# A fused attention, routing and two-layer MoE kernel: early weight chunks, index columns by matmul, and MoE2 in groups of 512 tokens

## The chip, the cores and the metric

The kernel runs on one core of one Trainium2 chip. The metric is the time of one execution in microseconds (us) of device time; several executions are timed, and their median counts. A profile of one execution shows what each engine did: PE (TensorE, the matmuls) with PEld (its weight loads), DVE (VectorE), ACT (ScalarE), POOL (GpSimd), SP (SyncE, which here only issues DMAs) and the DMA engines.

## The reference

Three stages follow each other on 2304 tokens (4 sequences of 576) of 512 features. The first is a sliding-window attention with 8 heads of 64 and a linear bias, whose window is 128 positions. The second sends every token to one of 8 experts, with at most 288 tokens per expert, in the order of the gate's values; the expert is a two-layer network. The third is a dense two-layer network with x * sigmoid(x) between.

```python
def _moe_ref(x, w_gate, w1, w2):
    N, D = x.shape                      # 2304, 512
    cap = N // E                        # 288
    logits = x @ w_gate
    order = np.argsort(-logits.flatten())
    ...                                 # greedy: best (token, expert) pair first, an expert takes cap tokens
    for e in range(E):
        mask = assigned == e
        h = np.maximum(x[mask] @ w1[e], 0.0)
        out[mask] = h @ w2[e]

def _moe2_ref(x, w_in, w_out):          # 512 x 2048, 2048 x 512
    h = x @ w_in
    g = h * (1.0 / (1.0 + np.exp(-h)))
    return g @ w_out
```

All of it is float32. Where the matmuls need the precision, the kernel splits an operand in two (a rounded part, `hi`, and the remainder, `lo`) and adds three products: hi x hi, hi x lo and lo x hi. One such product is one matmul instruction in the type fp32r.

## The kernel before, in words

**Order.** The kernel is written as one stream of operations and a scheduler puts them in an order on each engine, by its own estimate of the times. An operation may move ahead of earlier ones when its data and buffers are ready. `keep_in_program_order` (the `keep` in the code) holds an instruction behind the one written before it on its engine. Each engine and SP's queue then work strictly in the order that the scheduler fixed, and an instruction that waits holds everything behind it.

**Attention** (L80 to L265) goes over 18 tiles `t` of 128 tokens, each in two halves `g` of four heads, 36 halves `2t + g`. For each half, PE makes the scores, DVE adds the bias and takes the maximum, ACT makes the exponentials, PE transposes them (L240), ACT copies them out (L242), POOL selects the two parts of the window (`pp` and `pc`, L246 and L248), and PE multiplies with the values (L255). DVE normalises (L258 to L261) and the tile goes to the DRAM table `xtab` (L263). At the end of each tile `first_choices` (L47) makes, on DVE, the columns `fb` and `gt` (L69, L71) that a matmul (L74) adds up for the routing.

**Routing** (L333) finds the thresholds by a chain of small operations, mostly on DVE with short matmuls between; L384 is one of the wider. Dummy matmuls (`k.busy`, L309) run beside. `slots` (L496) ends in `idx96`: 24 columns of 96 token numbers, in the order of the experts' slots. `pi` is the PSUM tile that holds them before the addition of a constant.

**Weights** (L541). MoE1 has 64 chunks of 128 x 1024 float32 (512 KB), one for each expert and each eighth of the hidden features; `fetch` loads a chunk into one of four `raw` buffers (L559, on SP), casts it on ACT (L561) and subtracts on POOL (chunks 0 to 6) or DVE (L562) into one of five `ring` buffers. The first four chunks are fetched between the attention and the routing, their cast and subtraction held in program order. MoE2 has 16 chunks that come as int64, 1 MB each; `fetch64` (L566) loads each in two halves and unpacks them with five DVE operations and two ACT operations a half (L577 to L584). Nine of these are unpacked during MoE1 into the pool `keep`, two near its end into the ring, five during the first block of MoE2.

**MoE1** (L625). For each expert, three indirect DMAs on POOL gather 96 tokens each from `xtab` (L639), PE transposes them and they are split. For each of 8 slices `f` of hidden features there are 12 matmuls into `p` (L659) and 12 into the four accumulators `y0` to `y3` (L589 to L591), each of 288 columns. When an expert is done its four accumulators are copied to `yT`, which keeps all of y^T in SBUF (L680, L682). At expert 2, `by128` (L821) writes `idx96` to the DRAM table `itab` and reads it back as `idx128`, the same numbers in 18 columns of 128, which the output's scatter needs.

**MoE2** (L711) goes over nine blocks of 256 tokens. `split_block` (L601) splits a block of `yT`. A step `f` (16 a block) has 12 matmuls of 256 columns (`part0`, L617), the sigmoid on ACT (L761), a multiplication on DVE (L762), the cast on ACT (L771), the subtraction on DVE (L772), and, one step later, six matmuls of 512 columns into two of the four accumulators (L721). A finished block is copied out (L729, L731) and scattered to the output by token number (L733). The accumulators of even and odd blocks take different PSUM banks.

## Time and profile before

| what | value |
|---|---|
| median of 3 runs | 839.61 us (838.45 to 839.8) |
| the profiled execution's own time | 844.54 us |
| its span, first to last instruction | 842.8 us |
| DMA traffic | 90.32 MB in 34795 packets, 9184 of them under 512 bytes |
| HBM read and written | 79.87 MB and 9.45 MB |
| mean granted clock of PE | 0.979 |

The span is roughly: attention to 156 us, routing to 192 us, the first gather to 200 us, MoE1 to about 430 us, MoE2 to 833 us, and the last scatter. Each row of the views below gives an engine, a line of the code, what is written and what is read (`out<-in`), and the shape. A row of the stretches has PE, PEld, DVE, ACT and POOL, each as busy time with its number of instructions. The clock is the share of full speed that PE was granted.

Two things help in reading. Matmuls are pipelined, so the distance between their starts is their cost and not the length of one; and a busy PE can still be slow, so the number of matmuls in a stretch of known pace says more than the busy time.

### The profile page before, as it was taken

The page shows a single profiled execution, that of the slowest core. Times are in us where ns is not written, and L with a number is a line of the kernel's source. Part 1 is how long each engine was busy: PE and PEld are TensorE (multiplying, and loading weights), DVE is VectorE, ACT ScalarE, POOL GpSimd, SP SyncE. Part 2 cuts the span into 40 slices and gives each one's busy share as a digit, 9 for nine tenths or more (in the row PEclk, how much of TensorE's full clock was granted, in tenths as well). Part 3 has the DMA queues.
Part 4 walks back from the last instruction along what each step waited for, and adds up shares of the span by engine and source line. Part 5 has one row for each costly group of instructions (what it writes and reads, how often), then busy time and mean ns, then how long its engine had stood idle before and what let it go on. Part 6 is the DMA issues. An engine that isn't in the chain of part 4 may idle for free.

```text
span 842.8 us, 14810 instructions
## 1 busy us (share of the span) xinstructions
PE 802.4 (95%) x5599; PEld 734.5 (87%) x5599; DVE 495.1 (59%) x1325; ACT 368.4 (44%) x773; POOL 191.0 (23%) x202
## 2 busy tenths in 40 slices
PE   7989999688999699999999999999999999999997
PEld 5889999447999699999997899999999999999996
DVE  7978898772786487888799733234333333333332
ACT  4857776302554365555554423223332323232222
POOL 3869797604202002000003300000000000000000
PEclk8999999997999799999999999999999999999999
DMA  9997782312678677766434100000000000000000
GB/s 228 278 254 213 203 230 80 117 35 80 213 241 122 182 245 226 226 209 228 140 118 127 57 18 5 21 1 26 1 26 1 26 1 26 2 26 1 23 4 25
DMA packets 34795, 90.32 MB, mean 107 GB/s; under 512 B 9184, under 2 KB 9824, under 8 KB 34720
## 3 DMA queue, kind: packets, MB, share of 16 engines
q1 hardware_dynamic: 31744, 79.89, 33.1%
q0 software_dynamic: 2976, 9.44, 3.7%
q8 instruction: 46, 0.75, 0.4%
q14 instruction: 29, 0.24, 0.1%
HBM read 79.87 MB, written 9.45 MB: 106 GB/s over the span
## 4 chain that ended last, share of the span: by engine, by line
PE 56%; DVE 9%; DMA 8%; issue 2%; ACT 2%; POOLq 0%; ACTq 0%; SPq 0%
PE y L721 21%; DMA raw<-w 8%; PE p L659 6%; PE p L589 4%; PE p L591 4%; PE p L590 4%; PE pt L589 4%; PE pt L590 4%; PE pt L591 4%; DVE w L562 2%; PE y L590 2%; PE y L591 2%; PE y L589 2%; DVE bits L579 2%; DVE bits L578 1%
## 5 line engine op out<-in xcount | busy, mean ns | idle before, releaser
L721 PE MATMUL y<-w,gh 128*128 128x512 f32 x548 | 192.4, 395 | 0.1
L772 DVE TENSOR_TENSOR gl<-s,gh 128x256 fp32r<-128x256 f32 x137 | 60.1, 439 | 90.1 <-ACT gh L771 89.3
L721 PE MATMUL y<-w,gl 128*128 128x512 f32 x274 | 108.4, 396 | 2.1 <-DVE gl L772 1.7
L721 PEld LDWEIGHTS y<-w,gh 128*128 128x128 f32 x548 | 94.8, 190 | 10.1 <-ACT gh L771 0.8
L771 ACT CAST gh<-s 128x256 fp32r<-128x256 f32 x137 | 55.5, 407 | 96.5 <-PE y L721 69.3
L733 POOL DMA_INDIRECT out<-raw,idx x18 | 17.4, 966 | 344.2 <-ACT raw L731 323.0
L561 ACT CAST w<-raw 128x1024 fp32r<-128x1024 f32 x64 | 66.9, 1049 | 64.8 <-DMA raw<-w 45.0
L562 DVE TENSOR_TENSOR w<-raw,w 128x1024 fp32r<-128x1024 f32 x57 | 69.6, 1222 | 36.7 <-ACT w L561 36.7
L659 PE MATMUL p<-xh,w 128*128 128x288 f32 x512 | 81.6, 300 | 8.1 <-DVE hl L663 7.8
L659 PEld LDWEIGHTS p<-xh,w 128*128 128x128 f32 x512 | 72.0, 190 | 9.9 <-DVE hl L663 9.7
L590 PE MATMUL y<-hl,w 128*128 128x288 f32 x256 | 75.2, 298 | 0.0
L591 PE MATMUL y<-hh,w 128*128 128x288 f32 x256 | 74.7, 297 | 0.0
L589 PE MATMUL y<-hh,w 128*128 128x288 f32 x256 | 70.6, 301 | 0.0
L762 DVE TENSOR_TENSOR s<-p,s 128x256 f32<-128x256 f32 x72 | 30.5, 423 | 66.2 <-ACT s L761 66.1
L762 DVE TENSOR_TENSOR s<-pt,s 128x256 f32<-128x256 f32 x72 | 30.4, 423 | 63.6 <-ACT s L761 61.4
L721 PEld LDWEIGHTS y<-w,gl 128*128 128x128 f32 x274 | 51.5, 188 | 12.7 <-DVE gl L772 3.8
L761 ACT ACTIVATE s<-p 128x256 f32<-128x256 f32 x72 | 27.6, 384 | 72.9 <-PE p L591 66.1
L761 ACT ACTIVATE s<-pt 128x256 f32<-128x256 f32 x72 | 27.6, 384 | 70.2 <-PE pt L591 66.4
L232 ACT ACTIVATE pe<-sc,mx 128x128 f32<-128x128 f32 x144 | 47.6, 394 | 18.8 <-DVE mx L230 18.5
L639 POOL DMA_INDIRECT xg<-xtab,idx x24 | 26.2, 1092 | 128.1 <-PE pt L643 122.7
L255 PE MATMUL po<-va,pp 128*128 128x73 f32 x256 | 49.1, 274 | 0.5 <-DVE m L51 0.4
L255 PE MATMUL po<-va,pc 128*128 128x73 f32 x256 | 49.4, 275 | 0.0
(205 smaller groups left out, 2148.2 us busy)
## 6 DMA issues: line engine op xcount, KB each, us to landing
raw<-w SPq DMA_DIRECT2D x96, 512.0 KB, 4.1
kr<-kT SPq DMA_DIRECT2D x35, 256.0 KB, 5.0
va<-vA SPq DMA_DIRECT2D x18, 292.0 KB, 5.2
qr<-qT SPq DMA_DIRECT2D x18, 256.0 KB, 5.8
vt<-vT SPq DMA_DIRECT2D x18, 256.0 KB, 5.2
xtab<-xt SPq DMA_DIRECT2D x18, 256.0 KB, 4.8
xg<-xtab,idx POOLq DMA_INDIRECT x24, 4.7
out<-raw,idx POOLq DMA_INDIRECT x18, 2.7
```

Of the source, the lines that this page charges most:

```text
L255: nc.tensor.matmul(po[:, j, :], w[:, j, :], va[:, s, 4 * g + j, :], start=(i == 0), stop=(i == nb - 1))
L561: keep(nc.scalar.copy(hi, r))
L562: keep((nc.vector if i > 6 else nc.gpsimd).tensor_tensor(lo, r, hi, ALU.subtract))
L589: nc.tensor.matmul(out, whi, xhi, start=start, stop=False)
L590: nc.tensor.matmul(out, whi, xlo, start=False, stop=False)
L591: nc.tensor.matmul(out, wlo, xhi, start=False, stop=stop)
L659: nc.tensor.matmul(p, w[:, dc * P:dc * P + P], x[:, dc, :], start=(i + dc == 0), stop=(i == 2 and dc == DC - 1))
L721: mm = nc.tensor.matmul(a, g[:, w], x[:, 512:], start=(f + i == 0), stop=(f == FC2 - 1 and i == 2))
L761: nc.scalar.activation(s, p, AF.Sigmoid)
L762: nc.vector.tensor_tensor(s, p, s, ALU.mult)
L771: nc.scalar.copy(gh, s)
L772: nc.vector.tensor_tensor(gl, s, gh, ALU.subtract)
```

## The change

Four things change.

The first four chunks of MoE1 are loaded by `load_early` (written into tiles 12 to 15 of the attention) and split by `split_early` (written behind the halves 31 to 34, cast on ACT and subtraction on POOL, in program order). All other chunks are subtracted on DVE. The fifth is fetched at the start of MoE1.

`by128` no longer goes through DRAM. `slots` copies `pi` to `cent` (float16) on ACT, a constant `shift` (96 x 288) is loaded and copied at the end of the attention, and six matmuls of 6 columns move the 96-row columns into 128-row columns; one DVE operation adds the constant.

y^T is no longer kept in SBUF. The copies of an expert's accumulators go to `yo`, and one DMA on SP writes it to the DRAM tensor `yd`. `load_group` reads a group of 512 tokens back, and `split_group` splits it in four parts. The group after the current one is read at the start of each group.

MoE2 runs over four groups of 512 tokens and one of 256. `part0` has 12 matmuls of 512 columns; for each step there are 12 matmuls of 512 columns into all four accumulators (6 in the last group). The accumulators have one set of banks. Nine int64 chunks are unpacked in MoE1, and seven (`LATE`) in the first group of MoE2, all subtractions on DVE.

```diff
+EARLY = (31, 32, 33, 34)
...
+        if NT - 6 <= t < NT - 2:
+            wts.load_early()
...
             next(later)
+            if 2 * t + g in EARLY:
+                wts.split_early()
...
+        nc.scalar.copy(k.cent, pi)
         nc.vector.tensor_scalar_add(idx96, pi, float(N // 2))
...
+    def load_early(self):
+        r = self.raw.tile([P, 1024], F32, name="raw")
+        self.tc.nc.sync.dma_start(r, self.w32[self.next + len(self.raws)])
+        self.raws.append(r)
+
+    def split_early(self):
+        nc, keep = self.tc.nc, self.tc.keep_in_program_order
+        r = self.raws.pop(0)
+        hi, lo = self.parts(self.ring)
+        keep(nc.scalar.copy(hi, r))
+        keep(nc.gpsimd.tensor_tensor(lo, r, hi, ALU.subtract))
+        self.ready[self.next] = hi, lo
+        self.next += 1
...
-            keep((nc.vector if i > 6 else nc.gpsimd).tensor_tensor(lo, r, hi, ALU.subtract))
+            nc.vector.tensor_tensor(lo, r, hi, ALU.subtract)
...
-            (nc.vector if i < 11 else nc.gpsimd).tensor_tensor(lo[:, s], f, hi[:, s], ALU.subtract)
+            nc.vector.tensor_tensor(lo[:, s], f, hi[:, s], ALU.subtract)
...
-BT = 256
-NB = N // BT
+BT = 512
+GROUPS = [(o, min(BT, N - o)) for o in range(0, N, BT)]
 LAG = 7
-LATE = (0, 2, 4, 6, 8)
+SOON = 9
+LATE = (0, 1, 3, 4, 6, 7, 9)
...
+def load_group(tc, pool, yd, g, width=BT):
+    o, n = GROUPS[g]
+    r = pool.tile([P, DC, width], F32, name="yr", bufs=1)
+    tc.nc.sync.dma_start(r[:, :, :n], yd.rearrange("c p n -> p c n")[:, :, o:o + n])
+    return r
+
+def split_group(tc, pool, r, g):
+    o, n = GROUPS[g]
+    yh, yl = (pool.tile([P, DC, BT], F32R, name=x, bufs=1)[:, :, :n] for x in ("yh", "yl"))
+    for c in range(DC):
+        tc.nc.scalar.copy(yh[:, c], r[:, c, :n])
+        tc.nc.vector.tensor_tensor(yl[:, c], r[:, c, :n], yh[:, c], ALU.subtract)
+    return yh, yl
...
             if f == FC1 - 1:
+                yo = m1.tile([P, DC, CAP], F32, name="yo", bufs=1)
                 for d in range(DC):
...
+                nc.sync.dma_start(yd.rearrange("c p n -> p c n")[:, :, e * CAP:(e + 1) * CAP], yo)
+        wts.fetch(5)
         gather(0)
...
-                if n + 3 >= E * FC1 and 9 + n + 3 - E * FC1 < FC2 - len(LATE):
-                    wts.fetch64(9 + n + 3 - E * FC1, wts.ring)
...
+                if e == E - 1 and f == 1:
+                    r0 = load_group(tc, yg, yd, 0)
                 if e == E - 1 and f == 3:
-                    y0 = split_block(tc, [...], yT, 0)
+                    y0 = split_group(tc, yg, r0, 0)
...
-                accs[b] = [py.tile([P, 512], F32, name=f"y{b % 2 * 2 + d}") for d in range(2)]
+                accs[g] = [py.tile([P, 512], F32, name=f"y{d}") for d in range(nd)]
...
+                yh, yl = split_group(tc, m2 if g % 2 else yg, r, g)
+            if g < last_g:
+                r = load_group(tc, yg, yd, g + 1)
...
-                s = m2.tile([P, BT], F32, name="s")
+                s = m2.tile([P, n], F32, name="s", bufs=1)
...
-    def by128():
-        tc.keep_in_program_order(nc.sync.dma_start(itab.rearrange("(j r) o -> r (j o)", r=JR), idx96))
-        nc.sync.dma_start(idx128, itab.rearrange("(c p) o -> p (c o)", p=P))
+    def by128(pi):
+        cent = k.cent.rearrange("r (a i) -> r i a", i=4)
+        for b in range(3):
+            first = True
+            for i in range(4):
+                d = JR * i - P * b
+                if -JR < d < P:
+                    nc.tensor.matmul(pi[:, b, :], k.shift[:, JR - d:JR - d + P], cent[:, i, :], start=first, stop=not first)
+                    first = False
+        nc.vector.tensor_scalar_add(idx128.rearrange("p (a b) -> p a b", b=3), pi.rearrange("p b a -> p a b"), float(N // 2))
```

More of the change, by code (lines that the diff above doesn't have):

```diff
@@ L708, in moe1, with moe2, part @@
     return y0, p0
-def moe2(tc, wts, yT, y0, p0, idx128, out, ph, py, px):
+def moe2(tc, wts, yd, yg, y0, p0, idx128, out, ph, py, px):
     nc = tc.nc
+    last_g = len(GROUPS) - 1
     with tc.tile_pool(name="last", bufs=2) as last, tc.tile_pool(name="m2", bufs=2) as m2:
         accs = {}
-        def half(b, f, gh, gl, d):
+        def part(g, f, gh, gl, d):
             hi, lo = wts.ready[E * FC1 + f]
-            a, w = accs[b][d], slice(d * P, d * P + P)
-            late = b == NB - 1 and f >= FC2 - LAG
-            for i, (g, x) in enumerate(((gh, hi), (gl, hi), (gh, lo))):
-                mm = nc.tensor.matmul(a, g[:, w], x[:, 512:], start=(f + i == 0), stop=(f == FC2 - 1 and i == 2))
+            a, w = accs[g][d], slice(d * P, d * P + P)
+            late = g == last_g and f >= FC2 - LAG
+            for i, (x, y) in enumerate(((gh, hi), (gl, hi), (gh, lo))):
+                mm = nc.tensor.matmul(a, x[:, w], y[:, 512:], start=(f + i == 0), stop=(f == FC2 - 1 and i == 2))
                 if late:
@@ L724, in half @@
             if f == FC2 - 1:
-                if d == 0:
-                    accs[b, "out"] = wts.raw.tile([P, 2, 512], F32, name="raw")
-                ob = accs[b, "out"][:, d]
-                if d and b < NB - 1:
+                if d % 2 == 0:
+                    accs[g, "out"] = wts.raw.tile([P, 2, 512], F32, name="raw")
+                ob = accs[g, "out"][:, d % 2]
+                if d % 2 and g < last_g:
                     nc.vector.tensor_copy(ob, a)
@@ L747, in moe2 @@
-        pend, spare = None, []
-        for b in range(NB):
-            if b == 0:
+                accs[g] = [py.tile([P, 512], F32, name=f"y{d}") for d in range(nd)]
+            for d in range(nd):
+                if d and g == last_g and f >= FC2 - LAG:
+                    lag.append((g, f, gh, gl, d))
+                else:
+                    part(g, f, gh, gl, d)
+        pend, spare, step = None, [], 0
+        for g, (o, n) in enumerate(GROUPS):
+            if g == 0:
                 yh, yl = y0
@@ L804, in fused @@
         with ExitStack() as c2:
-            attention(c2, tc, qT, kT, vA, vT, wg, rel, k, xtab, X0, X, pgb)
+            attention(c2, tc, qT, kT, vA, vT, wg, rel, k, xtab, X0, X, pgb, wts)
             k.prepare(tc)
```

92 lines of the change are left out of this document (42 added, 50 removed).

## The prediction

> **What bounds the kernel now.** I read the page first (engine shares, clock), then the busy time by stretches, then the waits, then the chain that ended last. The first two rows are from the page; in the rows of the stretches the first number after the times is PE busy with its instructions, and the last three are the granted clock, the DMA share and GB/s.
>
> ```profile
> span 842.8 us, 14810 instructions
> PE 802.4 (95%) x5599; PEld 734.5 (87%) x5599; DVE 495.1 (59%) x1325; ACT 368.4 (44%) x773; POOL 191.0 (23%) x202
> ...
> 240.00:260.00 20.00, 20.00 (x156) 20.00 (x155) 16.76 (x27) 12.76 (x22) 2.50 (x2) 1.00 0.70 232
> 260.00:280.00 20.00, 14.69 (x115) 14.46 (x113) 8.78 (x14) 5.06 (x8) 2.36 (x2) 0.94 0.90 90
> 280.00:300.00 20.00, 17.88 (x111) 16.99 (x112) 14.36 (x24) 10.73 (x19) 3.19 (x3) 0.80 0.76 248
> 300.00:320.00 20.00, 20.00 (x156) 20.00 (x155) 17.08 (x26) 11.92 (x19) 0.84 (x1) 1.00 0.73 230
> ...
> 440.00:460.00 20.00, 18.17 (x108) 15.64 (x107) 19.38 (x32) 9.83 (x22) 7.98 (x5) 1.00 0.42 127
> 460.00:480.00 20.00, 19.34 (x116) 16.01 (x115) 17.47 (x32) 9.87 (x23) 7.14 (x5) 1.00 0.20 65
> 480.00:500.00 20.00, 20.00 (x128) 18.09 (x127) 7.56 (x17) 6.82 (x16) 1.98 (x2) 1.00 0.07 27
> ```
>
> TensorE is the bound from 200 us on: MoE1 issues 156 matmuls in 20 us at full pace, MoE2 128. So the counts say where time is lost. Between 260 and 300 us 226 came instead of 312: 86 x 0.128 = 11.0 us. Between 440 and 480 us 224 came instead of 256: 32 x 0.156 = 5.0 us, with DVE busy for 36.9 of 40 us. Outside these, MoE1 and MoE2 run at their matmul pace, and only fewer or better-shaped matmuls help there. Before 200 us lies the routing, a chain on DVE.
>
> **Early weight split.** Rows of the timeline: start, length, instruction, and in brackets the engine's idle time before it.
>
> ```profile
> 29.98 3.40 SPq L559 DMA_DIRECT2D raw<-w  x4
> ...
> 129.82 0.22 DVE L69 TENSOR_SCALAR fb<-X,m 128x8 bf16<-128x8 f32 x1
> 129.95 0.38 DVE L71 TENSOR_SCALAR gt<-cst,m 128x319 bf16<-128x319 f32 x1
> ...
> 144.16 0.64 POOL L246 TENSOR_SCALAR_AFFINE_SELECT pp<-pt 128x512 f32<-128x512 f32 x1 [1.75 <-ACT pt L242]
> ...
> 150.57 0.63 POOL L246 TENSOR_SCALAR_AFFINE_SELECT pp<-pt 128x512 f32<-128x512 f32 x1 [1.93 <-ACT pt L242]
> 151.15 0.63 POOL L248 TENSOR_SCALAR_AFFINE_SELECT pc<-pt 128x512 f32<-128x512 f32 x1
> ...
> 152.81 3.87 ACT L561 CAST w<-raw 128x1024 fp32r<-128x1024 f32 x4
> ...
> 153.39 0.44 PE L255 MATMUL po<-va,pc 128*128 128x73 f32 x2
> ...
> 156.53 11.94 POOL L562 TENSOR_TENSOR w<-raw,w 128x1024 fp32r<-128x1024 f32 x5
> 156.55 2.35 DVE L69 TENSOR_SCALAR fb<-X,m 128x8 bf16<-128x8 f32 x1
> 158.81 2.54 DVE L71 TENSOR_SCALAR gt<-cst,m 128x319 bf16<-128x319 f32 x1
> 166.64 1.99 DVE L384 TENSOR_TENSOR nC<-X,m 128x144 bf16<-128x144 f32 x1
> 174.60 0.31 DVE L384 TENSOR_TENSOR nC<-X,m 128x144 bf16<-128x144 f32 x1
> ```
>
> While POOL subtracts the five first chunks (156.5 to 168.5 us, 2.4 us each), three DVE instructions at the head of the routing take as long as a POOL instruction and not their own time: L69 2.35 for 0.22, L71 2.54 for 0.38, L384 1.99 for 0.31. Nothing covers them; the routing hangs on each. Removing them is worth 2.13 + 2.16 + 1.68 = 6.0 us. Chunk 4, now subtracted by DVE, can land in the gaps of the attention's end; if it falls into the routing it costs up to one L562 on DVE, 1.2 us (row further down).
>
> The four subtractions go behind halves 31 to 34 of the attention, that is, between the POOL selects that the last matmuls wait for. POOL has three gaps there, of 1.75 us (the first) to 1.93 (the last), some 5.5 together, each shorter than 2.4 us, so the selects slip: four times 2.4 is 9.6 us of POOL work against these, 4.1 us late at worst. The last selects end at 151.8 us and their matmuls start only at 153.4 us, so some 1.6 us is slack. That leaves 2.5 us late; I take 2.0 us lost (bounds 0 and 4.1), because the fourth subtraction can still fall behind the last select. The ACT casts (3.87 us for four) go among ACT's copies, for which POOL waits in two of these gaps; a cast between can cost its 1 us, which the 2.0 includes. The loads of the first four chunks left SP at 30 us already and need not move. Net gain 4.0 us.
>
> The Trainium skill's page "SBUF — State Buffer", section "SBUF: two separate sides", says that VectorE and GpSimd share a port pair as an exclusive lock, held for the whole instruction; the rows agree (a 0.22 us instruction took 2.35). By it the stall would move with the subtractions instead of going.
>
> **Index columns by matmul.** The two 4-byte-grained DMAs through DRAM (itab) go; six small matmuls, one ACT copy and one DVE addition come.
>
> ```profile
> 260.88 0.57 SPq L822 DMA_DIRECT2D itab<-idx  x1
> 276.07 0.39 SPq L823 DMA_DIRECT2D idx<-itab  x1
> ...
> 261.63 16.86 DMA raw<-w
> ...
> itab<-idx SPq DMA_DIRECT2D x1, 9.0 KB, 15.2
> ...
> PE p L659 <- DVE hl L663: 7.8, 3, 7.2
> ...
> L528 PE MATMUL pi<-OJ,OR 128*96 128x24 f16 x18 | 1.8, 228 | 3.2 <-POOLq L812 3.0
> ```
>
> SP issues the table's write at 260.88 us and its read, which waits for it, at 276.07; no weight chunk is issued in between but the one at 261.63, and that lands after 16.86 us instead of a median of 4.1 (row below, with y). PE stands for 7.2 us and then runs at a clock of 0.80. All of that is the 11.0 us counted above, and no other transfer explains it. The six new matmuls cost at most the 228 ns of L528 each, 1.4 us, or nothing if they fill a gap; I take 0.6. What is late next: weights at 156 matmuls per 20 us as in the stretches on both sides, so nothing. Gain 10.4 us.
>
> **MoE2 in groups of 512.** Rows of the chain (start, length) and of the groups by line (the first of these, L562, belongs to chunk 4 above):
>
> ```profile
> 575.53 2.28 PE y L721 x10
> 755.73 2.28 PE y L721 x10
> 750.89 1.39 PE y L721 x6
> ...
> L562 DVE TENSOR_TENSOR w<-raw,w 128x1024 fp32r<-128x1024 f32 x57 | 69.6, 1222 | 36.7 <-ACT w L561 36.7
> L729 DVE COPY raw<-y 128x512 f32<-128x512 f32 x8 | 5.5, 692 | 8.5 <-PE y L721 8.5
> L577 DVE TENSOR_SCALAR bits<-raw 128x512 int32<-128x512 int32 x32 | 13.4, 420 | 2.5 <-DMA raw<-w 2.5
> L578 DVE SCALAR_TENSOR_TENSOR bits<-raw,bits 128x512 int32<-128x512 int32 x32 | 21.9, 684 | 0.0
> L579 DVE SCALAR_TENSOR_TENSOR bits<-raw,bits 128x512 int32<-128x512 int32 x32 | 28.0, 879 | 0.2
> L582 DVE SCALAR_TENSOR_TENSOR f<-f,bits 128x512 f32<-128x512 f32 x32 | 21.8, 682 | 0.1
> L584 DVE TENSOR_TENSOR w<-f,w 128x512 fp32r<-128x512 f32 x22 | 15.1, 685 | 1.6 <-ACT w L583 1.6
> ```
>
> The pattern at 575.53 repeats at 755.73 four blocks of 16 steps later: 180.2 / 64 = 2.816 us a step. Its six 512-column matmuls take 1.390 (row at 750.89), so the twelve of 256 columns take 0.1188 each. A step of a 512 group is 24 matmuls of 0.2317 = 5.561 us against 2 x 2.816 = 5.632: 0.071 us saved, 64 steps, 4.5 us. The last group of 256 is as before. Bounds: 0, if a 512-column matmul with y as its moving operand costs two of 256, and 10.2 us at the 0.228 of the row at 575.53. The Trainium skill's page "TensorE: Matmul & The Clock Gate", section "Back-to-back issue gap", gives N/2.4 + 2.5 ns for a matmul at full clock; that would be 768 x 2.5 ns = 1.9 us here, an estimate from the page, but the rows stand above it (0.1188 for its 0.109), so I go by the rows.
>
> The start of MoE2 is the open part. Seven int64 chunks instead of five are now unpacked during MoE2, none in the last steps of MoE1, and all of it on DVE. A chunk is twice L577 to L584, 2 x 3.35 = 6.7 us; a step at 512 columns needs about 0.69 + 0.69 us (an estimate from L729 and L584, the rows of that width). Ten steps with seven chunks: 60.7 us of DVE work in 55.6 us. That overruns by 5.1 us, but chunk 15 is needed only in step 15, at 83 us, by when DVE has 69 us to do; and from a step's first matmuls to its use there are now 5.6 us instead of 2.8, for four operations of 0.7 at most. So I expect half of the 5.0 us lost there to go: gain 2.5, bounds +5.0 and -5.1 (all of the overrun shows). The accumulators lose their second set of banks; their copies (0.69) hide behind twelve matmuls of the next group (2.8 us), and would cost 4 x 0.7 without.
>
> **y through DRAM.** The copies of y^T stay and only change their target. New are eight writes of 0.59 MB on SP, each waiting for copies, and five reads. Reads are issued a group (88 us) ahead. Behind a waiting write stand weight loads, and behind these PE. SP's queue stood still for 15.2 us at L822 and PE lost 11.0, so about 4 us is covered. xtab's 256 KB landed in 4.8 us:
>
> ```profile
> raw<-w SPq DMA_DIRECT2D x96, 512.0 KB, 4.1
> xtab<-xt SPq DMA_DIRECT2D x18, 256.0 KB, 4.8
> ```
>
> A write waits for copies at the end of a planned step and its place on SP is planned with them, so most is covered; I take 2.0 us lost over the eight, bounds 0 and 6.
>
> **Sum.** 4.0 + 10.4 + 4.5 + 2.5 - 2.0 = 19.4 us. The profiled execution took 844.5 us (842.8 of span, the rest around it): 825.1. The median of the runs without that profile is 839.6, and the stages are the same, so 820.2.
>
> **Rivals.** (1) The cover holds everywhere: no slip in the attention (+2.0), none by the writes (+2.0), no stall in MoE2's first group (+2.5): 813.7. For it: slack of 1.6 and 4 us; against: DVE's 60.7 in 55.6. (2) DVE takes the lead in the first group: 2.5 becomes -5.1, 827.8. For it: 440 to 480 us, where DVE at 92% cost 5.0; against: the doubled slack. (3) The lock moves: DVE instructions of tiles 16 and 17 wait for the 9.6 us of POOL, the removed 6.0 is outweighed by 3.6, 7.6 below the 4.0: 827.8. For it: L69 as above; against: the selects' slack of 1.6 us, and that tile 17's own L69 and L71 come after all four. (4) Half of the hole at 260 us returns, because weights run just in time anyway: 825.7. Against it: full counts on both sides. (5) On the other side: the writes of y^T take the place of the table. If SP's queue waits for the landing of each, not only for copies, it stands for some 8 us (an estimate from xtab's 4.8 for under half the bytes); what exceeds the covered 4.2 costs PE its length, 8 x 3.8 = 30 us: 848. It decides from 6.9 us per write, where 21.4 us eats the gain. For it: L823 waited for a landing on this very queue; against: no instruction that follows a write at once reads what it wrote, until the last expert. The Trainium skill's page "DMA: Bandwidth & Descriptors", section "Anatomy of one DMA — SWDGE (gpsimd) path", says that a semaphore wait of a DMA happens on the issuing sequencer; the row of L823 agrees, and (5) hangs on it.
>
> **Chances.** Forecast 0.46, (1) 0.18, (2) 0.14, (3) 0.07, (4) 0.07, (5) 0.08, of which 0.02 with holds so near 6.9 us that nothing is left. A measurement of this kernel tells about 0.2% (1.7 us) from no change: faster 0.92, same 0.02, slower 0.06. The range 810 to 831 takes in the cases (1) to (4) with the bounds of the matmul price and of the writes, and leaves out (5).
>
> **What the new profile would show.** L69, L71 and L384 at 0.2 to 0.4 us right after the attention, and the attention ending within 2 us of 156.5; no interval of SP above 5 us in MoE1 and 156 matmuls in each 20 us where 115 and 111 stood; 512-column matmuls about 0.232 us apart through MoE2 with a step of 5.56; counts in MoE2's first 50 us short by some 2.5 us. Wrong would be: pitches of 0.238; selects on POOL that hold PE for over 4 us; waits of SP on y's copies followed by late weight casts.

## The result, and the profile after

| kernel | median | lowest to highest | ratio to before, 95% interval |
|---|---|---|---|
| before | 839.7 us, 4 runs | 838.45 to 841.22 | |
| after | 815.51 us, 4 runs | 809.65 to 819.76 | 0.9706 (0.9644 to 0.9769) |

The change makes the kernel 24 us faster; 820.2 was predicted. The profiled execution of the changed kernel took 815.47 us, its span is 813.8 us. That is 29.0 us below the profiled execution before, which lay 4.8 us above the median.

The page of the changed kernel, span and busy time of each engine:

```profile
span 813.8 us, 12971 instructions
...
PE 788.8 (97%) x4837; PEld 697.1 (86%) x4837; DVE 473.4 (58%) x1222; ACT 348.9 (43%) x658; POOL 168.1 (21%) x189
```

The trace has 762 matmuls fewer and 13.6 us less of busy PE; the other 15 of the 29.0 us were idle time of PE. The busy time of the changed kernel by stretches (the stretch and its length, then PE, PEld, DVE, ACT and POOL busy with their instructions, PE's clock, DMA share, GB/s):

```profile
140.00:150.00 10.00, 8.30 (x53) 7.71 (x52) 7.35 (x22) 8.21 (x18) 10.00 (x10) 0.78 0.54 150
150.00:160.00 10.00, 10.00 (x44) 8.75 (x44) 3.62 (x18) 0.00 (x0) 2.74 (x4) 0.50 0.47 166
...
260.00:280.00 20.00, 20.00 (x162) 19.93 (x161) 16.76 (x28) 13.07 (x22) 2.54 (x4) 1.00 0.89 298
280.00:300.00 20.00, 20.00 (x156) 20.00 (x155) 17.26 (x28) 11.54 (x20) 2.91 (x3) 1.00 0.83 277
...
440.00:460.00 20.00, 20.00 (x90) 16.57 (x89) 19.92 (x37) 12.32 (x21) 0.00 (x0) 1.00 0.46 156
460.00:480.00 20.00, 20.00 (x90) 16.57 (x89) 17.13 (x29) 8.06 (x15) 0.00 (x0) 1.00 0.10 29
480.00:500.00 20.00, 20.00 (x90) 16.53 (x90) 8.24 (x13) 6.91 (x13) 0.00 (x0) 1.00 0.00 1
```

Read these against the rows of before. The hole at 260 to 300 us is gone: 318 matmuls instead of 226, six of them the new small ones. From 440 us on, at the start of MoE2, DVE is as full as it was (19.92 of 20), but PE issues its 90 matmuls there as it does later, at 480 us. The rows at 140 and 150 us are new trouble: PE counts as busy, yet it issues 53 and then 44 matmuls, where the kernel before issues about 90 in 10 us, at a clock of 0.78 and 0.50. Before, no stretch of the attention's last 30 us had a clock below 1.00.

The timeline of the changed kernel shows where that begins and how the routing and the gather then stand (start, length, engine, line, what is written and read):

```profile
134.34 0.19 POOL L270 COPY X<-X 128x8 f32<-128x8 f32 x1
...
137.30 2.36 POOL L575 TENSOR_TENSOR w<-raw,w 128x1024 fp32r<-128x1024 f32 x1
...
140.80 2.36 POOL L575 TENSOR_TENSOR w<-raw,w 128x1024 fp32r<-128x1024 f32 x1
...
140.77 2.57 DVE L71 TENSOR_SCALAR gt<-cst,m 128x319 bf16<-128x319 f32 x1
...
160.18 0.23 DVE L69 TENSOR_SCALAR fb<-X,m 128x8 bf16<-128x8 f32 x1
160.32 0.38 DVE L71 TENSOR_SCALAR gt<-cst,m 128x319 bf16<-128x319 f32 x1
...
165.70 0.31 DVE L393 TENSOR_TENSOR nC<-X,m 128x144 bf16<-128x144 f32 x1
...
190.02 1.14 POOL L675 DMA_INDIRECT xg<-xtab,idx  x1 [3.78 <-DVEq L856]
...
198.32 2.38 PE L695 MATMUL p<-xh,w 128*128 128x288 f32 x16
```

L69, L71 and L393 (the old L384) have their own length again at the head of the routing. From the last L69 to the first gather it takes 29.84 us instead of 35.85 (156.55 to 192.40): 6.0 us less. But the stretch in front of it has grown. From the copy of tile 14's X (134.34, before 138.23) to the last L69 it takes 25.84 us, before 18.32. Behind the subtraction at 140.80 stands one L71 for 2.57 us, PE waits 1.7 us for it, and then its clock falls. The selects on POOL come 2.3 to 4.7 us later than before, counted from the copy of tile 14's X, but no wait of PE is put down to them. The only wait of PE in the changed kernel between 130 and 170 us (us in all, times, longest):

```profile
PE pgb L74 <- DVE gt L71: 1.7, 1, 1.7
```

And its stretches of 1 us around it:

```profile
142.00:143.00 1.00, 0.00 (x0) 0.00 (x0) 1.00 (x1) 1.00 (x2) 1.00 (x1) 1.00 0.77 266
...
145.00:146.00 1.00, 1.00 (x8) 0.74 (x8) 0.71 (x7) 0.95 (x3) 1.00 (x1) 0.80 1.02 422
146.00:147.00 1.00, 1.00 (x6) 0.95 (x5) 0.67 (x3) 1.00 (x2) 1.00 (x2) 0.50 0.10 37
```

The chain of the changed kernel (start, length, what) gives the pace of MoE2: a step is 529.61 to 535.05, 5.44 us, and its second product takes 2.72 us, 226.7 ns for each matmul of 512 columns. Before, a step of 512 tokens' worth took 5.632.

```profile
529.61 2.72 PE y L761 x12
...
535.05 2.72 PE y L761 x12
```

In SP's waits between 185 and 430 us the writes of y are new:

```profile
SPq L719 <- DVE yo L716: 23.7, 8, 9.2
```

The eight writes stood 23.7 us in its queue, each until the accumulators were copied. PE has 571 matmuls from 320 to 400 us, where the kernel before has 597.

The account of the two profiled executions, in us: start of the attention -3.9, its end +7.5, routing -6.0, hole at 260 us -11.0 (by the counts), 26 matmuls fewer at 320 to 400 us at 0.13 each, +3.4; start of MoE2 -5.9 (by the distances of matmul starts over their usual spacing, 420 to 480 us), the pace of MoE2 64 x 0.192 = -12.3. The sum is -28.2, of 29.0.

### The profile page after: what moved, and what is told of

The parts are those of the page before. It is cut to its first block, busy times and chain, and to the rows that moved or that the text cites. A ratio compares the mean times of both kernels' runs of the same rounds, so it can differ in the third digit from the quotient of the medians.

```text
span 813.8 us, 12971 instructions
## 1 busy us (share of the span) xinstructions
PE 788.8 (97%) x4837; PEld 697.1 (86%) x4837; DVE 473.4 (58%) x1222; ACT 348.9 (43%) x658; POOL 168.1 (21%) x189
## 4 chain that ended last, share of the span: by engine, by line
PE 68%; DMA 4%; DVE 2%; ACT 1%; issue 1%; POOLq 0%; ACTq 0%
PE y L761 24%; PE p L695 9%; PE p L616 4%; PE p L614 4%; PE p L615 4%; PE pt L616 4%; PE pt L614 4%; PE pt L615 4%; DMA raw<-w 4%; PE y L615 3%; PE y L614 3%; PE y L616 3%; DVE w L587 1%; ACT w L586 1%; PE pt L679 1%; PE p L318 1%
## 5 line engine op out<-in xcount | busy, mean ns | idle before, releaser
L761 PE MATMUL y<-w,gh 128*128 128x512 f32 x548 | 180.8, 389 | 0.0
L587 DVE TENSOR_TENSOR w<-raw,w 128x1024 fp32r<-128x1024 f32 x60 | 73.3, 1222 | 37.1 <-ACT w L586 37.0
L805 DVE TENSOR_TENSOR s<-pt,s 128x512 f32<-128x512 f32 (+1 forms) x40 | 25.5, 637 | 92.4 <-ACT s L804 92.4
L805 DVE TENSOR_TENSOR s<-p,s 128x512 f32<-128x512 f32 (+1 forms) x40 | 25.5, 636 | 91.4 <-ACT s L804 91.4
L815 DVE TENSOR_TENSOR gl<-s,gh 128x512 fp32r<-128x512 f32 (+1 forms) x73 | 48.0, 658 | 42.8 <-ACT gh L814 42.7
L814 ACT CAST gh<-s 128x512 fp32r<-128x512 f32 (+1 forms) x73 | 43.4, 595 | 55.3 <-DVE s L805 38.3
L804 ACT ACTIVATE s<-pt 128x512 f32<-128x512 f32 (+1 forms) x40 | 22.2, 555 | 101.8 <-PE pt L616 97.2
L804 ACT ACTIVATE s<-p 128x512 f32<-128x512 f32 (+1 forms) x40 | 22.2, 555 | 98.6 <-PE p L616 94.0
L615 PE MATMUL pt<-yl,w 128*128 128x512 f32 (+1 forms) x160 | 58.8, 368 | 0.0
L614 PE MATMUL p<-yh,w 128*128 128x512 f32 (+1 forms) x160 | 58.8, 368 | 0.0
L614 PE MATMUL pt<-yh,w 128*128 128x512 f32 (+1 forms) x160 | 58.8, 368 | 0.0
L616 PE MATMUL pt<-yh,w 128*128 128x512 f32 (+1 forms) x160 | 58.8, 368 | 0.0
```

The costliest lines, as they stand in the source:

```text
L587: nc.vector.tensor_tensor(lo, r, hi, ALU.subtract)
L614: nc.tensor.matmul(out, whi, xhi, start=start, stop=False)
L615: nc.tensor.matmul(out, whi, xlo, start=False, stop=False)
L616: nc.tensor.matmul(out, wlo, xhi, start=False, stop=stop)
L761: mm = nc.tensor.matmul(a, x[:, w], y[:, 512:], start=(f + i == 0), stop=(f == FC2 - 1 and i == 2))
L804: nc.scalar.activation(s, p, AF.Sigmoid)
```

## Experiments

### Three places for the early split

*after_again* is the changed kernel once more, for its spread. *late_split* undoes the early part: the chunks are loaded early as in the changed kernel, but all four are split behind the attention.

```diff
@@ attention
-            if 2 * t + g in EARLY:
-                wts.split_early()
@@ behind the attention
+        for i in range(4):
+            wts.split_early()
```

*pool_halves* cuts each early subtraction in two, *gap_split* leaves the casts in the attention and puts the subtractions on DVE behind the routing, into the time in which PE waits for the first gather.

```diff
@@ pool_halves
-        keep(nc.gpsimd.tensor_tensor(lo, r, hi, ALU.subtract))
+        for s in (slice(0, 512), slice(512, 1024)):
+            keep(nc.gpsimd.tensor_tensor(lo[:, s], r[:, s], hi[:, s], ALU.subtract))
@@ gap_split
-        keep(nc.gpsimd.tensor_tensor(lo, r, hi, ALU.subtract))
+        self.subs = getattr(self, "subs", []) + [(lo, r, hi)]
...
+        mark = m1.tile([1, 1], I32, name="mark")
+        nc.vector.tensor_copy(mark, idx96[0:1, 0:1])
+        for lo, r, hi in wts.subs:
+            tc.keep_in_program_order(nc.vector.tensor_tensor(lo, r, hi, ALU.subtract))
         wts.fetch(5)
```

> The changed kernel once more, for its spread. Theory A (the last attention tiles lose time when a POOL subtraction holds the DVE instruction L71, the matmul L74 behind it stops PE, and PE's clock falls to half until the routing): a second profile shows L74 waiting over 1 us for L71 and a granted clock near 0.5 before the routing, 815 us within 5, and the times of single runs spread by some 8 us as the clock falls or does not. Rival B (the spread lies elsewhere, in the weight stream of MoE1): the stretch before the routing is the same in both profiles and matmul counts in MoE1 differ.

> The early split alone undone: the four chunks are cast and subtracted on POOL behind the attention as before, the rest of the change stays. The traces say that the edit took 6.0 us out of the routing (L69, L71, L384 beside POOL) and put 7.5 us into the last three tiles. Theory A: the attention's end comes 7.5 us earlier, the routing gets 6 us longer, 814 us (1.5 faster than the changed kernel). Rival (the prediction's own sum: the edit gains 4.0): 819.5 us.

> Each early subtraction on POOL is cut into two of 512 columns, in the same places: POOL's work and the delay of its selects stay, but a DVE instruction that meets one waits for 1.2 us at most instead of 2.4. Theory A (the lock on L71 starts the loss): L74 waits under 0.8 us, the clock holds better, 3 to 6 us of the 7.5 come back, 810 to 812. Rival C (the selects are late, the lock is beside the point): the last selects are as late as in the changed kernel and so is the attention's end, 815 us, or some 0.5 us more for four more instructions.

> The four casts stay in the attention, but the four subtractions run on DVE behind the routing, while the first gather is under way and DVE has some 7 us free (4 x 1.22 us of work). Theory A and rival C both give back the 7.5 us of the last tiles and keep the routing free: 808 us, with the attention ending before 153 us. Rival D (the raw buffers of the four chunks come free 50 us later, so chunks 4 to 7 leave SP only at 193 us): PE waits for chunk 4 or 5 in MoE1's first 20 us, 812 us or more.

| kernel | median (lowest to highest) | ratio to before, 95% interval | tile 14's X to last L69 | last L69 to gather | gather to first matmul of MoE1 |
|---|---|---|---|---|---|
| after_again | 814.51 us (813.33 to 818.0) | 0.9694 (0.9629 to 0.9758) | 25.92 | 29.66 | 8.66 |
| late_split | 813.04 us (811.07 to 814.65) | 0.9654 (0.9592 to 0.9717) | 18.25 | 35.44 | 8.69 |
| pool_halves | 812.08 us (812.0 to 814.68) | 0.9661 (0.9599 to 0.9723) | 23.54 | 30.12 | 8.34 |
| gap_split | 814.69 us (813.27 to 816.49) | 0.9685 (0.9622 to 0.9747) | 18.10 | 28.27 | 14.34 |

Four medians within 2.6 us, with overlapping intervals: in time these places can't be told apart. In the traces they can, because each pays about the same elsewhere.

*after_again* repeats Theory A's stop: L74 waits 1.7 us for L71 once more, and the clock falls at 146 us. But its four times spread by 4.7 us and not by 8, and Rival B's sign is there too: the stretch before the routing is the same in both profiles (25.84 and 25.92 us), and the matmul counts of MoE1 differ (571 and 596 from 320 to 400 us). So the stop and the clock are in both, and the 2.1 us by which the second profiled execution is faster are gained in MoE1.

The rows of *late_split*'s timeline show the old lock back at the head of the routing:

```profile
154.50 9.59 POOL L573 TENSOR_TENSOR w<-raw,w 128x1024 fp32r<-128x1024 f32 x4
...
154.52 2.35 DVE L69 TENSOR_SCALAR fb<-X,m 128x8 bf16<-128x8 f32 x1
...
156.78 2.54 DVE L71 TENSOR_SCALAR gt<-cst,m 128x319 bf16<-128x319 f32 x1
```

So the early split gains 6 us in the routing and loses 7.5 in the attention. *pool_halves* confirms the lock, since one L71 shrinks from 2.57 to 1.48 us with the piece of POOL that it stands behind, but it gets back only 2.3 of the 7.5 us, where Theory A expected 3 to 6; the rest of its waits and its later fall of the clock stay. Even the 2.3 can't be credited to the halves: *yd_act* (below) has the changed kernel's attention with its whole pieces, and there the stretch takes 23.42 us, with the clock low from 149 to 159 us and not from 146 to 162.

In *gap_split* the attention and the routing give all that was hoped, and the gather is issued at 182.68 instead of 190.02 us; then 6 us go in the gather. The casts alone, which it leaves in the attention, cost nothing there: 18.10 us against *late_split*'s 18.25. Its timeline:

```profile
182.65 4.61 DVE L724 TENSOR_TENSOR w<-raw,w 128x1024 fp32r<-128x1024 f32 x4
182.68 2.19 POOL L675 DMA_INDIRECT xg<-xtab,idx  x1 [3.78 <-DVEq L860]
183.91 3.73 SPq L584 DMA_DIRECT2D raw<-w  x4
...
185.17 1.75 POOL L675 DMA_INDIRECT xg<-xtab,idx  x1 [0.31 <-issue]
```

And PE's waits between 180 and 200 us:

```profile
PE pt L679 <- DMA xg<-xtab,idx: 5.0, 3, 2.4
```

The first two issues on POOL take 2.19 and 1.75 us beside DVE's subtractions, not 1.14 and 0.92. Each subtraction that ends frees a raw buffer, and SP at once issues the next load of 512 KB: 2 MB stand among the gathered rows, for which PE then waits. Two causes are seen here together; *gap2* below takes both away. Rival D's time comes, but not its cause, PE waiting for chunk 4 or 5: in the first 20 us of MoE1 PE waits for gathered rows alone.

### The early subtractions on DVE in the attention

*dve_early* moves them from POOL to DVE in the same places. *spread* cuts them into quarters of 256 columns, one in each half tile from 17 on, with the four loads in tiles 7, 9, 11 and 13.

```diff
@@ dve_early
-        keep(nc.gpsimd.tensor_tensor(lo, r, hi, ALU.subtract))
+        keep(nc.vector.tensor_tensor(lo, r, hi, ALU.subtract))
@@ spread
+EARLY = range(17, 34)
+LOADS = (7, 9, 11, 13)
...
+                keep(nc.vector.tensor_tensor(lo[:, s], r[:, s], hi[:, s], ALU.subtract))
...
+                keep(nc.scalar.copy(hi[:, s], r[:, s]))
```

> The four early subtractions on DVE instead of POOL, in the same places of the attention. They take 1.1 to 1.2 us each there (the late ones of this form on DVE do), so DVE gets 4.6 us more work in its last two tiles but POOL and DVE no longer stand against each other. Theory A (the lock of POOL on L71 makes the PE wait and then run slow): L71 falls from 2.57 to some 0.4 to 0.6 us, the longest wait on L74 from 2.7 to under 1.5, the stretch from the last X copy of tile 14 to the last L69 from 25.9 to 19 to 22 us, and the kernel is 3 to 6 us faster than after: 809 to 811. Rival C (it is the late selects and the slow PE, whatever stands on POOL): the stretch stays at 24 to 26 us, or grows, because DVE is now what the selects wait for; 814 to 818.

> The early split taken apart: the four chunks are loaded in tiles 7, 9, 11 and 13 of the attention, and each is cast by ACT and subtracted by DVE in quarters of 256 columns, one quarter in each half tile from 17 on (the subtraction one half tile behind its cast); POOL has none of it. A quarter should take 0.33 to 0.4 us on DVE. Theory I (what the early split lost in the attention came from pieces of over 1 us in the tight chain of DVE and PE, on whichever engine, and from PE's clock after the stop they cause; pieces of a third of it fit in the slack of DVE): the stretch from tile 14's X copy to the last L69 is 18 to 19 us, the routing 28.3 to 29.8, the gather 8.3, and the kernel takes 814.5 less 7 to 9 = 805.5 to 807.5. Rival J (DVE, at 17 to 18.4 us of 20 in the attention, has no room for them): tiles 9 to 16 get longer, X14's copy comes at 137 to 140 us instead of 134 to 136, and the kernel takes 809 to 813.

Neither gains. *dve_early* takes 818.5 us (815.59 to 823.92, ratio 0.9719, 0.9655 to 0.9783), which can't be told from the changed kernel; its profiled execution is the slowest of the four. *spread* takes 826.26 us (825.1 to 828.59, ratio 0.9809, 0.9771 to 0.9848) and is slower. The times of A and I fall here. C's longer stretch comes, at 0.5 us above C's times; J's late copy comes too, but *spread* loses more than J's 809 to 813. The subtractions of *dve_early* among its groups by line between 130 and 165 us (busy time, mean ns of one, idle time before), then two of its stretches:

```profile
L575 DVE TENSOR_TENSOR w<-raw,w 128x1024 fp32r<-128x1024 f32 x4 | 5.6, 1410 | 0.0
```

```profile
144.00:145.00 1.00, 0.28 (x3) 0.07 (x1) 1.00 (x6) 0.00 (x0) 0.90 (x1) 1.00 0.52 176
...
147.00:148.00 1.00, 1.00 (x8) 0.98 (x8) 1.00 (x7) 1.00 (x4) 0.27 (x1) 0.55 0.70 287
```

The same group of *spread*, between 100 and 165 us:

```profile
L581 DVE TENSOR_TENSOR w<-raw,w 128x256 fp32r<-128x256 f32 x11 | 9.7, 880 | 0.1
```

In *dve_early* no L71 is held up (0.38 to 0.83 us), DVE is full from 141 to 149 us, PE stops at 144 to 145.4, and the clock falls as it does behind the lock. The stretch to the last L69 is 29.13 us. In *spread* a quarter takes 880 ns, over two thirds of the 1222 ns that a whole chunk took on DVE in MoE1 (L562 before). POOL is busy for 14 to 15 of each 20 us beside it from 100 to 140 us, so the lock is the likely reason. Tile 14's X comes at 148.4 us instead of 134 to 136. So in none of the places tried had the attention room for this work, on either engine. It is not the lock alone that costs: in *dve_early* no L71 is held, and the time is lost all the same. And every kernel that loses time in this stretch has PE's clock at 0.50 for 10 to 24 us in it, or across its end; *late_split*, *gap_split* and *gap2* keep 1.00 there.

### Parts of the change undone

*g256* takes MoE2 back to groups of 256 tokens, with the turn of accumulators and the loading places that belong to it; all else, y through DRAM too, is as in the changed kernel. *itab* brings back the DRAM table for the index columns. *first_256* keeps groups of 512 and issues only the first product in two passes of 256 columns.

```diff
@@ g256
-BT = 512
+BT = 256
-LATE = (0, 1, 3, 4, 6, 7, 9)
+LATE = (0, 2, 4, 6, 8)
...
-                accs[g] = [py.tile([P, 512], F32, name=f"y{d}") for d in range(nd)]
+                accs[g] = [py.tile([P, 512], F32, name=f"y{g % 2 * 2 + d}") for d in range(nd)]
@@ itab
+        tc.keep_in_program_order(nc.sync.dma_start(itab.rearrange("(j r) o -> r (j o)", r=JR), idx96))
+        nc.sync.dma_start(idx128, itab.rearrange("(c p) o -> p (c o)", p=P))
@@ first_256
-    for dc in range(DC):
-        w = slice(dc * P, dc * P + P)
-        three(tc.nc, p, hi[:, w], lo[:, w], yh[:, dc, :], yl[:, dc, :], dc == 0, dc == DC - 1)
+    for h in range(0, p.shape[-1], 256):
+        c = slice(h, h + 256)
+        for dc in range(DC):
+            w = slice(dc * P, dc * P + P)
+            three(tc.nc, p[:, c], hi[:, w], lo[:, w], yh[:, dc, c], yl[:, dc, c], dc == 0, dc == DC - 1)
```

> The groups of MoE2 back at 256 tokens, with the two turns of accumulators, the loading places of the expert chunks and everything else as in the changed kernel (y goes through DRAM, index columns by matmul, early split). Theory E (the gain of MoE2 is that of fewer short matmuls: 64 steps of 512 tokens' worth at 226.6 ns a matmul of 512 against 2 x 117.3 or so with the first half's weights loaded twice, 12.4 us, and 5 to 6 at the start of MoE2, where splits by 256 stand in the way): 814.5 + 12 to 18 = 826 to 833, with the spacing of its 512-column matmuls back at 231 to 235 ns in the runs of 12 that follow a stretch of 256. Rival F (the gain in MoE2 comes from reading y back from DRAM, which spares the split's source or takes the copies out of the way, not from the width): under 820.

> The index columns of 128 through the DRAM table again, as in the kernel before, all else as in the changed kernel. Theory G (the 4-byte packets of that table's two transfers delay the weight chunk behind them, and PE stands for 11 us near 260 us): 814.5 + 9 to 12 = 823.5 to 826.5, with a hole at 255 to 270 us in which PE waits for L586 or L587 of a chunk whose load took over 15 us. Rival H (the hole of before came from the loading order of the 64 chunks and the ring, which the other parts changed too): 814 to 817, with the table's transfers under cover.

> The changed kernel with only the first product of MoE2 (part0) issued in two passes of 256 columns; groups, splits, accumulators, reads and the second product stay at 512 tokens. Theory O (the steady gain of MoE2 is that of the first product's matmul width: 24 of 256 columns at 119.1 ns stand for 12 of 512 at 226.6, 0.139 us a step, and the 512-column matmuls just behind a stretch of 256-column ones are slower, five of them by 5 ns, 0.026 us a step): 64 steps x 0.165 = 10.6 us more, 814.5 + 10.6 = 825, and the second product's spacing at 231 to 235 ns in the first five of each run of 12 and 226 to 227 from the sixth on. Rival P (the gain comes with the group: four accumulators, half as many splits and reads; the width of the first product matters little): 814 to 817 with the second product at 226.6 ns throughout.

| kernel | median (lowest to highest) | ratio to before, 95% interval | against after_again's 814.51 |
|---|---|---|---|
| g256 | 836.11 us (834.14 to 839.49) | 0.9960 (0.9940 to 0.9979) | +21.6 |
| itab | 827.42 us (826.03 to 828.99) | 0.9840 (0.9776 to 0.9903) | +12.9 |
| first_256 | 827.33 us (823.93 to 830.71) | 0.9850 (0.9808 to 0.9892) | +12.8 |

*itab* brings the hole back, by the stretches of its trace:

```profile
260.00:280.00 20.00, 11.73 (x92) 11.50 (x90) 7.94 (x12) 3.87 (x6) 1.91 (x2) 0.84 0.79 136
280.00:300.00 20.00, 15.38 (x98) 15.32 (x99) 16.04 (x27) 13.47 (x24) 2.10 (x2) 0.73 0.84 259
```

And by its DMA issues (KB each, us from issue to landing):

```profile
itab<-idx SPq DMA_DIRECT2D x1, 9.0 KB, 16.6
```

190 matmuls come in these 40 us where 318 come in the changed kernel. A table of 9 KB takes 16.6 us to land, and two transfers issued next to it land late. Theory G holds for the cause, and H falls, but the 12.9 us are not the hole of before alone. PE's longest wait, and what ACT waits for in it (rows of the waits and of the timeline):

```profile
PE y L613 <- ACT hh L697: 12.9, 1, 12.9
...
276.07 1.04 ACT L585 CAST w<-raw 128x1024 fp32r<-128x1024 f32 x1 [10.98 <-DMA raw<-w]
282.09 2.18 ACT L639 CAST yh<-yr 128x512 fp32r<-128x512 f32 x4 [4.97 <-DMA yr<-yd]
```

First the weight chunk is late, as in the kernel before; then ACT stands another 5 us for the first read of y from DRAM, which was issued at 263.98 us and landed 18.1 us later, and the instruction that PE needs comes behind it. In the changed kernel this read lands in 6.8 us. The kernel before has no such read.

*g256* lies above E's 12 to 18 us. Its steady pace is that of before: its rows below show six matmuls in 1.39 us, and it issues 642 between 520 and 620 us, where the kernel before has 641. That is 12.3 us. The other 9 us are at the start of MoE2, most of them in one wait of PE: 5.1 us for a multiplication on DVE, during which the clock falls (0.83 in the stretch from 420 to 440 us). Views of *g256*: the chain, PE's waits from 400 to 560 us, a row of the timeline, and two stretches.

```profile
530.05 1.39 PE y L763 x6
```

```profile
PE pt L614 <- DVE s L807: 5.1, 1, 5.1
```

```profile
422.32 0.38 ACT L806 ACTIVATE s<-pt 128x256 f32<-128x256 f32 x1 [3.04 <-DMA yd<-yo]
```

```profile
440.00:460.00 20.00, 19.18 (x119) 16.06 (x118) 19.94 (x42) 12.11 (x25) 0.00 (x0) 1.00 0.25 79
460.00:480.00 20.00, 20.00 (x127) 18.02 (x126) 9.35 (x22) 8.19 (x22) 1.97 (x2) 1.00 0.17 53
```

DVE is not behind in that wait: it stands idle for 4.15 us, because the sigmoid on ACT comes late, and the sigmoid waits for the last write of y to land (issued at 416.73 us, landed 5.5 us later). The changed kernel has the same wait on ACT, and PE has enough 512-column matmuls in front of it not to stop:

```profile
420.69 0.60 ACT L804 ACTIVATE s<-pt 128x512 f32<-128x512 f32 x1 [3.58 <-DMA yd<-yo]
```

So this wait belongs to y through DRAM, and the larger group hides it. From 440 to 480 us *g256* issues 246 matmuls, 10 short of 256, where the kernel before is 32 short. Most of what the kernel before loses there is therefore gone already at the old group size.

*first_256* takes the pace apart. Its chain:

```profile
523.19 2.75 PE y L763 x12
...
528.81 2.75 PE y L763 x12
```

A step is 5.62 us instead of 5.44, though only the first product was changed. Of the 0.18 us, 0.15 are the first product (2.87 us for 24 matmuls of 256 columns, 2.72 for 12 of 512) and 0.03 the second, 2.75 instead of 2.72. The starts in its trace between 520 and 740 us say why: the first five of the twelve stand 228.5 to 235.5 ns apart, from the sixth on 226.5 to 227. Before, these runs are short, mostly of two to six, so nearly every one stands among the first five: 1.39 us for six. Theory O holds; 64 x 0.18 = 11.5 us of the measured 12.8 are this, and P falls.

### The writes of y, and a second trace of before

*yd_act* issues the writes of y from ACT's queue (`nc.scalar.dma_start` for `nc.sync.dma_start` in that line).

> The eight stores of y issued by ACT instead of SP, nothing else. Theory K (a store on SP stands before the loads of the weight chunks until both accumulators are copied, which I put at 2.0 us in all): 812.5 to 813.5, with no wait of SP on the yo copies and the PE waits at 320 to 400 us gone. Rival L (the loads run far enough ahead, so the wait in SP's queue costs nothing): 814 to 815, the same PE waits.

813.55 us (810.27 to 814.86), ratio 0.9664 (0.9628 to 0.9699): between K and L in time. The stretches from 320 to 400 us, of *yd_act*, the changed kernel and *after_again*:

```profile
320.00:400.00 80.00, 79.52 (x594) 78.52 (x594) 62.18 (x97) 45.01 (x75) 0.92 (x1) 1.00 0.72 241
```

```profile
320.00:400.00 80.00, 77.09 (x571) 75.39 (x570) 62.13 (x96) 43.27 (x73) 1.12 (x1) 1.00 0.73 237
```

```profile
320.00:400.00 80.00, 79.67 (x596) 78.64 (x595) 63.58 (x98) 44.42 (x74) 1.01 (x1) 1.00 0.75 249
```

The same kernel loses 25 matmuls here in one execution and none in another, with the writes on SP in both. So the writes on SP cost PE nothing here in one execution; whether the 3.4 us of the other are theirs is not shown, and moving them is worth no more than the spread.

*before_again* was meant to tell whether the 3.9 us at the start of the attention belong to the change.

> A second profile of the kernel before. If its wait at 48 us (2.6 us of PE for the scaled q and k, whose loads came late) is of one execution, the last X copy of tile 14 comes at 134 to 136.5 us as in the changed kernels instead of 138.2, and the span is 838 to 840. If it belongs to the kernel, the copy is at 138 again and the changed kernel gained 3 to 4 us there by what it loads first. Theory either way: the routing from the last L69 to the gather takes 35.5 to 36.2 us, the stretch from that copy to the last L69 18.0 to 18.5.

Its single execution took 850.84 us, with PE's clock at 0.77 and 0.81 in the stretches from 20 to 60 us, and tile 14's X came at 141.99 us. The two figures that were to hold either way missed as well: 19.89 us from there to the last L69 and 38.60 on to the gather, with falls of the clock in both. It can't be compared, and the question stays open: the changed kernels have that copy at 133.6 to 136.3 us, except *spread*, which adds work in front of it, and *dve_early*, which is the same up to there and has it at 138.86.

### A better place: the subtractions behind the data

*gap2* is *gap_split* with both troubles of the gather taken away. The first subtraction waits for the first gathered rows, the others for the last low part of gather(0), each by a copy of one element; chunk 4 is fetched one step later.

```diff
+        mark = m1.tile([1, 2], F32, name="mark")
+        def behind(x, i, n):
+            tc.keep_in_program_order(nc.vector.tensor_copy(mark[:, i:i + 1], x))
+            for lo, r, hi in wts.subs[:n]:
+                tc.keep_in_program_order(nc.vector.tensor_tensor(lo, r, hi, ALU.subtract))
+            del wts.subs[:n]
...
+                if e + j == 0:
+                    behind(xg[0:1, 0:1], 0, 1)
...
         gather(0)
+        behind(xs[0][1][0:1, 0, CAP - 1:CAP].bitcast(F32), 1, 3)
-        wts.fetch(5)
```

> The casts of the four early chunks stay in the attention, as in gap_split, but their subtractions on DVE wait for data: the first for the first gathered rows (by a copy of one element of them), the other three for the last low part of gather(0). So none stands beside the descriptors of the gather on POOL, and the raw buffers come free, and the loads of chunks 4 to 7 start, only when those rows have landed. Theory M (gap_split lost its 7.3 us in the gather: 1.9 us by POOL's descriptors beside DVE, the rest by 2 MB of loads in front of the gathered rows): attention 18.1 and routing 28.3 us as in gap_split, the gather issued at 182 to 184 us, 8.3 to 9.5 us from there to the first L695, which then comes at 190.5 to 193, MoE1 as in the changed kernel, the kernel at 806 to 809. Rival N (DVE can't take three subtractions, the low part of h and chunk 4 within the first 10 us of MoE1, or chunk 4 comes late): first L695 as in M, but PE waits for L587, the new subtractions or L699 between 191 and 220 us, 4 us or more in all, and 811 to 814.

808.55 us (808.06 to 811.83), ratio 0.9632 (0.9583 to 0.9681): the lowest median of this study, 6.0 us below *after_again* and 7.0 below the changed kernel. The ratios' intervals overlap, so its lead is not clear of the spread. Its timeline:

```profile
135.29 0.19 POOL L270 COPY X<-X 128x8 f32<-128x8 f32 x1
...
153.40 0.23 DVE L69 TENSOR_SCALAR fb<-X,m 128x8 bf16<-128x8 f32 x1
...
181.66 1.14 POOL L675 DMA_INDIRECT xg<-xtab,idx  x1 [3.78 <-DVEq L866]
...
190.41 1.85 PE L697 MATMUL p<-xh,w 128*128 128x288 f32 x12
```

18.11 us of attention, 28.26 of routing, 8.75 of gather: 55.12 us where the changed kernel takes 63.98. Theory M holds in the traces and in the time. Of these 8.9 us about one is spent again at the start of MoE1, where PE waits 1.0 us for L701 at 195 us (N's trouble, in small).

## Why the prediction held, and where it did not

**Early weight split** (+4.0 predicted, -1.5 in the traces). The step "worth 2.13 + 2.16 + 1.68 = 6.0 us" is exact: 35.85 to 29.84. The step that failed is "I take 2.0 us lost (bounds 0 and 4.1)": 7.5 were lost, outside of its bounds. It counted POOL's work against the gaps between selects only. The selects did slip, but no wait of PE is put down to them. It left out that the instruction that holds PE up is DVE's L71, behind the second subtraction, and that PE's clock then falls to 0.50 until 162 us. Rival (3) had that lock, against which the prediction set that "tile 17's own L69 and L71 come after all four"; it was tile 15's that was caught. Its price of 7.6 us below the 4.0 was nearer than the forecast's, at a chance of 0.07. *late_split* puts the part at 1.5 us slower than its undoing, within the intervals.

**Index columns** (+10.4 predicted). 11.0 us in the trace, 12.9 by *itab*. The cause named (the fine-grained table among the weight loads) is shown by that run; its price there holds some 5 us of ACT's wait for a read of y, which the kernel before does not have. The new matmuls, L875, were put at 0.6 us; the six start between 260.5 and 260.7 us, 0.3 us in all.

**MoE2's pace** (+4.5 predicted, 12.3 in the traces). The mis-sized term is "24 matmuls of 0.2317": they are 0.2267 apart, and the gain lies above the bound of 10.2. The 0.2317 was the mean of runs of six behind matmuls of 256 columns, and the changed kernel has no such runs except in its last group. The row at 575.53, ten in 2.28 us, was the better guide, and the bound of 10.2 came from it; it too holds some that stand just behind narrower ones.

The rule that the prediction cites there, N/2.4 + 2.5 ns, has a cost for each matmul besides its columns, and the trace agrees in kind. In size it does not: 226.7 ns at 512 columns where the formula of the Trainium skill's page gives 215.8 (an estimate from the page), and 119.6 at 256 (*first_256*) where it gives 109.2. With the page's 2.4 columns a nanosecond the cost besides the columns is about 13 ns, and the measurement decides.

**MoE2's start** (+2.5 predicted, bounds +5.0 and -5.1). 5.9 us came back, all that was lost there, though DVE is at 19.92 of 20 us. The prediction weighed DVE's excess of work against the doubled slack. In *g256*, without the doubled slack, the distances of matmul starts over their usual spacing give 1.5 us and not 5.9, beside the wait for y's write and the slow clock behind it. So the doubled slack does not explain most of the gain. The prediction passed over that POOL subtracts beside DVE there in the kernel before (8.0 and 7.1 us of its time in the two stretches) and no longer does. The same operation on DVE from 440 to 480 us, before and then in the changed kernel:

```profile
L579 DVE SCALAR_TENSOR_TENSOR bits<-raw,bits 128x512 int32<-128x512 int32 x9 | 12.4, 1376 | 0.1
```

```profile
L604 DVE SCALAR_TENSOR_TENSOR bits<-raw,bits 128x512 int32<-128x512 int32 x11 | 7.4, 683 | 0.0
```

It looks like the lock of the early split again: the 879 ns with which the prediction priced this operation is a mean that holds these long ones. That the end of the lock brought the gain back is likely and not shown, because no run moves these subtractions alone.

**Writes of y** (-2.0 predicted). PE's shortfall beside them is 0 to 3.4 us by execution. Rival (5) did not come: SP waits for the landing of a write only in front of two reads (5.0 us in all), and *yd_act*, which takes the writes off SP, lies 1 us below *after_again*, within the spread. The sum had no term for the last write at the start of MoE2, on which the sigmoid waits 3.58 us; the 512-column matmuls cover it.

**Sum.** 19.4 was predicted against the medians' 24.2. The errors have opposite signs: 7.8 too little for the pace and 3.4 for MoE2's start, 5.5 too much for the split. So it is partly luck that the sum came this near. The time lies nearer to rival (1)'s 813.7, which is luck too: its full cover in the attention did not come. By the parts undone, 12.9 + 21.6 - 1.5 = 33 us is more than the whole 24.2, so the parts are not additive: in *itab* a read of y lands late, and in *g256* the last write of y is no longer covered. The kernel before has neither.

Of the signs that the prediction named, L69, L71 and L393 are short, and the counts at 260 us are full. Against it, the last L69 comes at 160.18 us and not within 2 us of 156.5, SP waits up to 9.2 us for y's copies, and MoE2's first 50 us are not short.

## What to carry to other kernels

Moving work off a critical chain pays only where the engines of the new place have room; four chunks' subtractions cost some 6 to 7.5 us at each of three places (attention, routing, gather), and were cheap only where they waited for the data that PE waited for too. A part that is undone alone can meet another part's new transfers; look at what PE waits for before taking the difference as its price. Before pricing an off-loaded instruction, look for the small instructions on the engine that shares its lock, and for the matmul that hangs on them. Take the price of a matmul from a long run of its own width, not from a mean over mixed runs.

## What the runs showed of the hardware that was not expected

**The clock after a short stop.** PE stops from 141.7 to 143.4 us in the changed kernel; its clock is 0.80 at 145 and 0.50 from 146 to 162 us, although PE is busy all that time. In *dve_early* it falls at 147 us, behind a stop that ends at 145.4. In *late_split* a stop of 0.4 us at 148 us leaves the clock at 1.00. In MoE1 and MoE2 longer stops left it at 1.00 too: 1.7 us at 457 us in the kernel before, and 2.3 us at 365 us in *dve_early*. The Trainium skill's page "TensorE: Matmul & The Clock Gate", section "What's actually happening", has the clock fall after an idle window of about 3.4 us; here it fell after a stop of half that length, so the measurement decides. But the length of a stop alone does not tell whether the clock falls. Which work around it does was not tried.

**Spacing after narrower matmuls.** Five matmuls of 512 columns behind a stretch of 256 columns are 2 to 9 ns slower each, then the spacing settles. The effect is shown by *first_256*; what causes it stays open.

**POOL's gather beside DVE.** The issue of an indirect DMA took 2.19 us instead of 1.14 beside DVE's subtractions (*gap_split*), and in *gap2* one took 2.01 instead of 0.92 beside a subtraction at 194.45 us. This fits the lock that held L71 behind POOL, working the other way.
